# Block-causal attention and a gated MLP on one core: query block 8 ahead of its period, MLP groups listed by period, a sixth x buffer

## The chip, the cores and the metric

The kernel runs on one NeuronCore of a Trainium2 chip. A core has five engines that run side by side, each through its own queue in order: TensorE (PE, matrix products, its weight loads are shown as PEld), VectorE (DVE), ScalarE (ACT), GpSimd (POOL) and SyncE (SP, which issues all DMAs here). They meet at semaphores. The metric is the time of one execution on the device in microseconds; less is better.

## The reference

Eight batches of eight heads with 576 tokens and head dimension 64. Attention with a block-causal mask (blocks of 64 tokens) gives x, and a gated MLP with a spatial product follows:

```python
scores = np.where(block_i >= block_j, scale * q @ k.T, -1e9)
attn = exp(scores - max) / (sum + 1e-9)
x = attn @ v                                   # 576 x 512 per batch
h = np.maximum(x @ w_in, 0.0)                  # 512 -> 1024
u, v = h[..., :512], h[..., 512:]
v_n = (v - mean(v)) / sqrt(var(v) + 1e-6)
v_s = w_spatial @ v_n + b_spatial              # over the tokens, 576 x 576
out = (u * v_s) @ w_out
```

## The kernel before

The MLP's products are made in three passes: each float32 operand is split into a rounded part and a remainder (`hi` and `lo`, `gh` and `gl`, `vh` and `vl`), and hi x hi, hi x lo and lo x hi are added up in PSUM.

Two heads make a pair, four pairs a batch: 32 pairs. The four pairs of batch 0 run first in an older form (lines 819 to 843, "boot"), while the weights are loaded and split in the background. From pair 4 on one pass of the loop at line 874 is a period: the attention of pair g, the values product of pair g-1, and a share of the MLP of an earlier batch. Four periods make a batch.

Parts of a period:

- `scores_8` (L509): query block 8, the last 64 tokens of both heads. Two products (L515) into two PSUM banks, then `top` (the scaled minimum with mask on DVE, L484; the exponential on ACT, L491), `norm` (sums on DVE, L499 and L502; scaling on POOL, L505) and `turn_blocks(…, 8, 0)`: three transposes on DVE (L574 to L576) from the buffer `p8` into `pb`.
- `scores_run` (L521): the other query blocks 3, 2, 1, 0 of both heads: eight products (L536), eight `top`, the `norm`s, and the first turn. "Block 3" below is the first read of a score bank by DVE in it (L484 with 128x512).
- `av_pair` (L596) of the pair before: two banks of products of the turned probabilities `ptt` with `v` (L606), each copied out as `hi` by ACT (L403) and `lo` by DVE (L404).
- `turn_blocks` (L561): 32 x 32 transposes on DVE (L581, L583) from the p buffers into `pb`; `regroup` (L585): four DMAs for each head that bring `pb` into `ptt` (L592). There is one `pb` and one `ptt`.
- MLP groups, each an accumulation on PE in one of two PSUM banks: `v_group` (five a batch: four of 128 tokens, L639, and the tail, L650; with a statistics chain on DVE and ACT in later steps, L661 to L700), `u_group` (eight, L710), `sp_group` (the spatial product and the gating, eight, L734 to L747; L741 is the product with u), `out_group` (eight, L760; a copy on ACT, L766, and an output DMA, L767).

Six PSUM banks go round (`bank`, L466): 2 for block 8, 6 for the scores, 2 for `av` in each period. So the first `av` bank is that of block 3, and `av` may start once DVE has read it.

The order is written out by hand: `in_order` (L235) ties every new instruction to the one before it on its engine, so each engine, SP too, runs in the order of the program. `issue` (L851) makes a group's first step (its products and first evacuation) and then one further step of each earlier group that has steps left. Which groups run in a period is a matter of credit: each period adds `G_PAIR` (13.3), each group takes its cost, and `group` (L861) issues while credit is left. The order of the groups of a batch is that of `order` at L773, with the first half's gating behind the u groups, one u group, its output groups, then the second half. In a period block 8 comes first, then one group, then `scores_run`, `av_pair`, one group, the other turns with both regroups, and the other groups.

The x of a pair lies in one of five buffers (`xt_p`, L83), from its `av` until the last u group of its batch. The p buffers are six of 576 columns (L81), the output tiles four (L86).

Of the kernel before, what the change touches and what calls it, by code (L numbers as in the profile page):

```python
# [10 lines left out]
F32 = mybir.dt.float32  # L11
# [6 lines left out]
P = 128  # L18
# [22 lines left out]

G_V, G_VT, G_U, G_SP, G_OUT = 2.75, 1.83, 1.60, 1.86, 1.60
G_PAIR = (4 * G_V + G_VT + 8 * (G_U + G_SP + G_OUT)) / 4

TILES = [(2, 4), (0, 0), (0, 1), (1, 0), (1, 1), (0, 2), (0, 3), (1, 2), (1, 3)]
NT = len(TILES)  # L50
# [5 lines left out]
def kernel(  # L56
# [21 lines left out]
    const = ctx.enter_context(tc.tile_pool(name="const", bufs=1))  # L78
    raw_p = ctx.enter_context(tc.tile_pool(name="raw_p", bufs=2))
    v_p = ctx.enter_context(tc.tile_pool(name="v_p", bufs=2))  # L80
    p_p = ctx.enter_context(tc.tile_pool(name="p_p", bufs=6))  # L81
    pt_p = ctx.enter_context(tc.tile_pool(name="pt_p", bufs=1))
    xt_p = ctx.enter_context(tc.tile_pool(name="xt_p", bufs=5))  # L83
    st_p = ctx.enter_context(tc.tile_pool(name="st_p", bufs=6))
    ff_p = ctx.enter_context(tc.tile_pool(name="ff_p", bufs=1))
    o_p = ctx.enter_context(tc.tile_pool(name="o_p", bufs=4))  # L86
    ps_s = ctx.enter_context(tc.tile_pool(name="ps_s", bufs=3, space=PSUM))
    ps_t = ctx.enter_context(tc.tile_pool(name="ps_t", bufs=2, space=PSUM))
    ps_av = ctx.enter_context(tc.tile_pool(name="ps_av", bufs=1, space=PSUM))
# [142 lines left out]
    def pass_over():  # L232
        seen[0] = len(traced.instructions)
# [27 lines left out]
    boot = []  # L261
    BOOT_TAGS = [f"v{x}{c}" for x in "hl" for c in range(FULL)]

    def p_tile(b, nm, n):

        if b == 0 and n <= DH:
            boot.append(nm)
            k = (len(boot) - 1) % (len(BOOT_TAGS) + 2)
            if k < len(BOOT_TAGS):
                t = ff_p.tile([P, DH], F32R, tag=BOOT_TAGS[k], name=f"p_{nm}")  # L270
                return t.bitcast(F32)
        return p_p.tile([P, S], F32, tag="p", name=f"p_{nm}")

    banks = []

# [7 lines left out]
    def scores(b, pr, i):  # L283
        hd, t = TILES[i]
        nm = f"{b}_{pr}_{i}"
        nmax = st_p.tile([P, 2], F32, tag="nmax", name=f"nmax_{nm}")
        if t != 1:
            sums[0] = st_p.tile([P, 4], F32, tag="ssum", name=f"ssum_{nm}")
        ssum = sums[0]
        sc = 1 if t == 1 else 0  # L290
        pt = p_tile(b, nm, P * (t + 1))
        if hd < 2:
            n = P * (t + 1)
            js = slice(64 * hd, 64 * hd + 64)
            qs = slice(S + t * P, S + (t + 1) * P)
            ps = s_bank(nm)
            raw = raws[(b, pr)]
            mm(ps[:, :n], raw[js, qs], raw[js, :n], start=True, stop=True)
            nc.vector.tensor_tensor_reduce(
                out=pt[:, :n], in0=ps[:, :n], in1=mask[:, 512 - n:], scale=-0.125, scalar=BIG,  # L300
                op0=ALU.add, op1=ALU.min, accum_out=nmax[:, 0:1],
            )
            mx = nmax[:, 0:1]
        else:
            n = S
            for z in range(2):
                zs = slice(z * HT, (z + 1) * HT)
                ps = s_bank(f"{nm}_{z}")
                raw = raws[(b, pr)]
                mm(ps[:, :HT], raw[:, Q8:], raw[:, zs], start=True, stop=True)  # L310
                nc.vector.tensor_tensor_reduce(
                    out=pt[:, zs], in0=ps[:, :HT], in1=mask[:, :HT], scale=-0.125,
                    scalar=BIG if z == 0 else nmax[:, 0:1],
                    op0=ALU.add, op1=ALU.min, accum_out=nmax[:, z:z + 1],
                )
            mx = nmax[:, 1:2]
        nc.scalar.activation(
            pt[:, :n], pt[:, :n], AF.Exp, bias=mx, scale=-1.0, accum_out=ssum[:, sc:sc + 1]
        )
        ptiles[(b, pr, i)] = pt  # L320
        if t == 0:
            return
        nc.vector.tensor_scalar(
            out=ssum[:, 0:sc + 1], in0=ssum[:, 0:sc + 1], scalar1=EPS_SM, scalar2=None, op0=ALU.add
        )
        nc.vector.reciprocal(ssum[:, 2:3 + sc], ssum[:, 0:sc + 1])
        for k in range(sc, -1, -1):
            pk = ptiles[(b, pr, i - k)]
            nk = n if k == 0 else n - P
            nc.gpsimd.tensor_scalar(  # L330
                out=pk[:, :nk], in0=pk[:, :nk], scalar1=ssum[:, 2 + sc - k:3 + sc - k],
                scalar2=1.0, op0=ALU.mult, op1=ALU.mult,
            )
# [175 lines left out]
    def scores_8(b, pr):  # L509
        raw = raws[(b, pr)]  # L510
        st = stats[(b, pr)] = st_p.tile([P, 32], F32, tag="sst", name=f"sst_{b}_{pr}", bufs=3)
        parts = []
        for z in range(2):
            ps = bank(f"s8_{b}_{pr}_{z}")
            mm(ps[:, :HT], raw[:, Q8:], raw[:, z * HT:(z + 1) * HT], start=True, stop=True)  # L515
            parts.append(ps[:, :HT])
        top(st, 8, 0, p8[:, :S], parts)
        norm(st, [(8, 0, p8[:, :S])])
        turn_blocks(b, pr, 8, 0)

    def scores_run(b, pr):  # L521


        raw = raws.pop((b, pr))
        st = stats.pop((b, pr))
        ps = {}
        for t in (3, 2, 1, 0):
            for hd in range(2):
                js = slice(64 * hd, 64 * hd + 64)
                n = P * (t + 1)  # L530
                if t:
                    bk = bank(f"s{t}_{b}_{pr}_{hd}")
                    ps[(t, hd)] = bk[:, :n]
                    if t == 1:
                        ps[(0, hd)] = bk[:, n:n + P]
                mm(  # L536
                    ps[(t, hd)], raw[js, S + t * P:S + (t + 1) * P], raw[js, :n],
                    start=True, stop=True,
                )
        due = None  # L540
        for ts in ((3,), (2,), (1, 0)):
            tiles = []
            for hd in range(2):
                p = p_p.tile([P, S], F32, tag="p", name=f"p{ts[0]}_{b}_{pr}_{hd}")
                at = 0
                for t in ts:
                    n = P * (t + 1)
                    p_of[(b, pr, t, hd)] = p[:, at:at + n]
                    top(st, t, hd, p[:, at:at + n], [ps[(t, hd)]])
                    tiles.append((t, hd, p[:, at:at + n]))  # L550
                    at += n
            if due:
                norm(st, due)
            due = tiles
        turn_blocks(b, pr, 3, 0)
        norm(st, due)
# [60 lines left out]
    def moe(b):  # L617
# [149 lines left out]
            nc.sync.dma_start(outT[b, es, z * HT:(z + 1) * HT], o)  # L767
            yield

        vs = [(G_V if c < FULL else G_VT, lambda c=c: v_group(c)) for c in (0, 1, FULL, 2, 3)]  # L770
        us = [(G_U, lambda z=z, d=d: u_group(z, d)) for z in range(2) for d in range(ND)]

        order = "vuvuvuvuvuuuu" if b else "vvvuvuvuuuuuu"  # L773
        groups = [(vs if w == "v" else us).pop(0) for w in order]

        groups = groups[:-1] + [(G_SP, lambda d=d: sp_group(0, d)) for d in range(ND)] + groups[-1:]
        groups += [(G_OUT, lambda e=e: out_group(0, e)) for e in range(NO)]
        groups += [(G_SP, lambda d=d: sp_group(1, d)) for d in range(ND)]
        groups += [(G_OUT, lambda e=e: out_group(1, e)) for e in range(NO)]
        return groups  # L780


    pairs = [(b, pr) for b in range(B) for pr in range(NPAIR)]
# [2 lines left out]
    def run(gen):  # L786
        for _ in gen:
            pass
# [55 lines left out]

    queue = moe(0)
    credit = 0.0
    behind = []

    def issue(f):  # L851

        gen = f()
        next(gen)
        for e in list(behind):
            if next(e, e) is e:
                behind.remove(e)
        behind.append(gen)
        in_order()

    def group():  # L861
        nonlocal credit, n
        if queue and credit > 0.0:
            t, f = queue.pop(0)
            credit -= t
            issue(f)
            step_background(n)
            pass_over()
            n += 1
            return True  # L870
        return False

    pass_over()
    for g in range(NPAIR, len(pairs)):
        b, pr = pairs[g]
        n = max(n, g * NT)
        credit += G_PAIR
        scores_8(b, pr)
        in_order()
        group()  # L880
        scores_run(b, pr)
        av = av_pair(*pairs[g - 1]) if g > NPAIR else iter([])
        next(av, None)
# [2 lines left out]
        next(av, None)  # L886
        turn_blocks(b, pr, 2, 0)
        in_order()
        if g > NPAIR and pr == 0:
            queue += moe(b - 1)  # L890
        group()
        turn_blocks(b, pr, 1, 0)
        turn_blocks(b, pr, 0, 0)
        regroup(b, pr, 0)
        turn_blocks(b, pr, 2, 1)
        turn_blocks(b, pr, 1, 1)
        turn_blocks(b, pr, 0, 1)
        regroup(b, pr, 1)
        in_order()
        while group():  # L900
            pass
        if g + 1 < len(pairs):
            load_v(*pairs[g + 1])
        if g + 2 < len(pairs):
            load_pair(*pairs[g + 2])
        in_order()
    while queue:
        issue(queue.pop(0)[1])
    run(av_pair(*pairs[-1]))
    for _, f in moe(B - 1):  # L910
        issue(f)
    for e in behind:
        run(e)
# [64 lines left out]
```

## Time and profile before

| | us |
|---|---|
| median of 3 runs | 846.97 |
| lowest, highest | 844.66, 847.73 |
| profiled execution | 844.37 |
| its span, first to last instruction | 842.5 |
| PE busy in the span | 724.4 |
| granted clock of PE, mean | 0.947 |

The span is what the profile shows; 1.9 us of the profiled execution lie outside it. Times in views are counted from the start of the span. A view of waits gives, for each instruction group, how long its engine stood idle before it and what ended that, by semaphore events; a wait for several is put down to the last. A row of a timeline has the start, the length, engine, line, operation, tiles written and read, shapes and, in brackets, the idle time before it with what ended it. Matmuls overlap in the pipeline, so their lengths are longer than the distance of their starts. SP's rows show the issue of a DMA, not its transfer.

### The profile page before, as it was taken

The numbers are of one execution on the slowest core, as the hardware profiler recorded it, in microseconds if no ns is written. First come the engines' busy times: TensorE is split into PE (matmuls) and PEld (weight loads), VectorE is DVE, ScalarE is ACT, GpSimd is POOL, SyncE is SP. The second block draws the span as 40 slices with busy tenths as digits, with TensorE's granted clock in tenths as the row PEclk, the third lists the DMA queues.
The fourth block names the chain that finished last, engine by engine and source line by source line (L and its number), as shares of the span: only waits on it lengthen the run. The fifth ranks groups of instructions, "written<-read, shape, count | busy, mean of one in ns | idle before, by whom it ended". The sixth has DMA issues, their size and how long they took to land. (4 is left out here: it accounts for less than half of the span.)

```text
span 842.5 us, 14409 instructions
## 1 busy us (share of the span) xinstructions
PE 724.4 (86%) x4864; PEld 616.2 (73%) x4864; DVE 483.8 (57%) x1755; ACT 386.2 (46%) x1088; POOL 277.7 (33%) x428
## 2 busy tenths in 40 slices
PE   9998788888887987979789888888898888888997
PEld 5555577777776866868678767777677776787887
DVE  6967864566545665455665555565545657445331
ACT  6776633355433554335533345334543346334441
POOL 5775343233413333222333213332132322323121
PEclk9999799999999989999899998999999998999999
DMA  5544444541455404554225543245443453443001
GB/s 195 165 140 125 128 124 118 137 130 45 124 152 151 125 15 110 152 153 124 52 81 145 153 123 82 78 129 150 114 123 72 129 142 87 124 106 93 32 8 49
DMA packets 53660, 94.42 MB, mean 112 GB/s; under 512 B 5970, under 2 KB 43346, under 8 KB 53588
## 3 DMA queue, kind: packets, MB, share of 16 engines
q1 hardware_dynamic: 53588, 93.52, 40.8%
q8 instruction: 38, 0.62, 0.3%
q14 instruction: 34, 0.28, 0.1%
HBM read 38.18 MB, written 9.44 MB: 57 GB/s over the span
## 5 line engine op out<-in xcount | busy, mean ns | idle before, releaser
L505 POOL TENSOR_SCALAR p<-p,sst 128x384 f32<-128x384 f32 (+4 forms) x252 | 137.5, 560 | 312.4 <-DVE sst L502 272.9
L491 ACT ACTIVATE p<-p,sst 128x384 f32<-128x384 f32 (+4 forms) x252 | 144.4, 575 | 145.6 <-DVE sst L484 145.6
L606 PE MATMUL av<-ptt,v 128*64 128x32 f32 (+4 forms) x1120 | 113.1, 366 | 53.9 <-DVE sst L484 45.7
L606 PEld LDWEIGHTS av<-ptt,v 128*64 128x64 f32 x1120 | 100.1, 168 | 69.0 <-DVE sst L484 59.1
L484 DVE CUSTOM_DVE_ANT_0 p<-s,mask 128x384 f32<-128x384 f32 (+4 forms) x252 | 108.1, 478 | 44.8 <-PE s L515 42.7
L710 PE MATMUL mu<-x,wi_hi 128*128 128x288 f32 x512 | 111.1, 298 | 1.4 <-ACT vr L644 1.4
L760 PE MATMUL mo<-gh,wo_hi 128*128 128x288 f32 x256 | 63.9, 323 | 38.6 <-DVE u L741 21.6
L741 DVE TENSOR_TENSOR u<-ms,u 128x288 f32<-128x288 f32 x64 | 27.9, 436 | 111.0 <-PE ms L739 111.0
L639 PE MATMUL mv<-wi_hi,x 128*128 128x512 f32 x256 | 89.1, 409 | 2.9 <-ACT vr L644 2.2
L581 DVE STREAM_TRANSPOSE pb<-p 128x384 f32<-128x384 f32 (+1 forms) x224 | 91.4, 448 | 0.0
L734 PE MATMUL ms<-ws_hi,vh 128*128 128x288 f32 x256 | 80.7, 315 | 9.0 <-ACT vh L689 7.7
L710 PEld LDWEIGHTS mu<-x,wi_hi 128*128 128x128 f32 x512 | 84.6, 188 | 3.5 <-ACT vr L644 1.9
L690 POOL TENSOR_TENSOR vl<-vr,vh 128x512 fp32r<-128x512 f32 x32 | 41.0, 1280 | 138.5 <-ACT vh L689 81.0
L734 PE MATMUL ms<-ws_hi,vl 128*128 128x288 f32 x256 | 76.2, 298 | 5.7 <-POOL vl L690 5.7
L760 PEld LDWEIGHTS mo<-gh,wo_hi 128*128 128x128 f32 x256 | 46.1, 208 | 45.0 <-issue 24.5
L734 PE MATMUL ms<-ws_lo,vh 128*128 128x288 f32 x256 | 75.3, 294 | 0.0
L710 PE MATMUL mu<-x,wi_lo 128*128 128x288 f32 x256 | 69.8, 295 | 0.0
L536 PE MATMUL s<-raw 64*128 64x512 f32 (+1 forms) x448 | 68.6, 443 | 0.0
L766 ACT COPY o<-mo 128x288 f32<-128x288 f32 x64 | 25.6, 400 | 93.7 <-PE mo L760 69.4
L536 PEld LDWEIGHTS s<-raw 64*128 64x128 f32 x448 | 41.2, 186 | 28.3 <-issue 19.3
L760 PE MATMUL mo<-gl,wo_hi 128*128 128x288 f32 x256 | 61.0, 322 | 0.0
L639 PEld LDWEIGHTS mv<-wi_hi,x 128*128 128x128 f32 x256 | 49.3, 193 | 14.9 <-ACT vr L644 2.4
(127 smaller groups left out, 1379.4 us busy)
## 6 DMA issues: line engine op xcount, KB each, us to landing
ptt<-pb SPq DMA_DIRECT2D x224, 200.0 KB, 4.1
raw<-qk SPq DMA_DIRECT2D x31, 608.0 KB, 5.2
v<-v SPq DMA_DIRECT2D x32, 320.0 KB, 4.0
outT<-o SPq DMA_DIRECT2D x64, 144.0 KB, 2.9
rwi<-w_in SPq DMA_DIRECT2D x8, 512.0 KB, 3.9
rwo<-w_out SPq DMA_DIRECT2D x4, 512.0 KB, 3.6
rws<-w_spT SPq DMA_DIRECT2D x4, 288.0 KB, 2.8
rwt<-w_spT SPq DMA_DIRECT2D x2, 144.0 KB, 2.8
```

Of the source, the lines that this page charges most:

```text
L484: nc.vector.tensor_tensor_reduce(out=p[:, at:at + n], in0=ps, in1=mk, scale=-0.125, scalar=BIG if m == 0 else st[:, k:k + 1], op0=ALU.add, ...
L491: nc.scalar.activation(p, p, AF.Exp, bias=mx, scale=-1.0, accum_out=st[:, 10 + k:11 + k])
L505: nc.gpsimd.tensor_scalar(out=p, in0=p, scalar1=st[:, k:k + 1], scalar2=1.0, op0=ALU.mult, op1=ALU.mult)
L536: mm(ps[(t, hd)], raw[js, S + t * P:S + (t + 1) * P], raw[js, :n], start=True, stop=True,)
L581: nc.vector.transpose(to(hd * XH + 32 * t, [[P, m], *dims] if m > 1 else dims), p[:, :m * P])
L606: mm(to[js, :, PA - C_N[c]:], vt[:, c, js], ptt[:, 2 * z:2 * z + 2, at:at + C_N[c]], start=(c == 0), stop=(c == 4),)
L639: mm(ps, xs[k][:, j, cs], w[:, k, DH:], start=(n == 0), stop=(n == 3 * NC - 1),)
L690: nc.gpsimd.tensor_tensor(out=vl, in0=vr, in1=vh.bitcast(F32), op=ALU.subtract)
L710: mm(ps[:, :HT], w[:, k, ds], xs[k][:, j, zs], start=(n == 0), stop=(n == 3 * NC - 1),)
L734: mm(ps[:, :HT], a[:, ds], w[:, k, zs], start=(n == 0), stop=False)
L741: nc.vector.tensor_tensor(out=uz, in0=ps[:, :HT], in1=uz, op=ALU.mult)
L760: mm(ps[:, :HT], w[:, k, es], a[:, k, :], start=(n == 0), stop=(n == 3 * ND - 1),)
```

## The change

Four things are changed.

1. `scores_8` becomes a generator of three steps: products and `top`; `norm`; the turn into `pb`. The next pair's block 8 takes one step behind each of the last four groups of a period (the fourth only ends the generator). The first pair's block 8 runs ahead of the loop.
2. `moe` returns five lists instead of one queue with costs. A period takes one of them; the first period of a batch takes the last list of the batch before it and the first of its own. The gating groups of a half end a period, and the output groups that use them begin the next. The other turns stand behind the first group, the two regroups behind the second and the third.
3. Six x buffers for five.
4. To make room: p buffers by size (two of 512, four of 384 columns), boot's block 8 in `p8`, boot's p tiles in a round of eleven for ten, three output tiles for four.

```diff
-    p_p = ctx.enter_context(tc.tile_pool(name="p_p", bufs=6))
+    p_p = ctx.enter_context(tc.tile_pool(name="p_p", bufs=1))
-    xt_p = ctx.enter_context(tc.tile_pool(name="xt_p", bufs=5))
+    xt_p = ctx.enter_context(tc.tile_pool(name="xt_p", bufs=6))
-    o_p = ctx.enter_context(tc.tile_pool(name="o_p", bufs=4))
+    o_p = ctx.enter_context(tc.tile_pool(name="o_p", bufs=3))
...
+    def p_big(nm):
+        return p_p.tile([P, 512], F32, tag="p3", name=nm, bufs=2)
+
+    def p_small(nm):
+        return p_p.tile([P, 384], F32, tag="p21", name=nm, bufs=4)
...
         top(st, 8, 0, p8[:, :S], parts)
+        yield
         norm(st, [(8, 0, p8[:, :S])])
+        yield
         turn_blocks(b, pr, 8, 0)
+        yield
...
-        order = "vuvuvuvuvuuuu" if b else "vvvuvuvuuuuuu"
-        groups = [(vs if w == "v" else us).pop(0) for w in order]
-
-        groups = groups[:-1] + [(G_SP, lambda d=d: sp_group(0, d)) for d in range(ND)] + groups[-1:]
...
+        if b == 0:
+            first = [[*vs[0:3], us[0], vs[4]], [vs[3], *us[1:6]], us[6:] + sp[0]]
+        else:
+            first = [
+                [vs[0], vs[4], us[0]], [vs[1], us[1], vs[2], us[2], vs[3], us[3]], us[4:] + sp[0]
+            ]
+        return [*first, out[0] + sp[1], out[1]]
...
     pass_over()
+    ahead = scores_8(*pairs[NPAIR])
+    run(ahead)
+    mlp = moe(0)
+    rest = []
     for g in range(NPAIR, len(pairs)):
         b, pr = pairs[g]
         n = max(n, g * NT)
-        credit += G_PAIR
-        scores_8(b, pr)
-        in_order()
-        group()
         scores_run(b, pr)
         av = av_pair(*pairs[g - 1]) if g > NPAIR else iter([])
...
         turn_blocks(b, pr, 2, 0)
         in_order()
-        if g > NPAIR and pr == 0:
-            queue += moe(b - 1)
-        group()
-        turn_blocks(b, pr, 1, 0)
-        turn_blocks(b, pr, 0, 0)
-        regroup(b, pr, 0)
-        turn_blocks(b, pr, 2, 1)
-        turn_blocks(b, pr, 1, 1)
-        turn_blocks(b, pr, 0, 1)
-        regroup(b, pr, 1)
+        if pr == 0:
+            if g > NPAIR:
+                mlp = moe(b - 1)
+            groups, rest = rest + mlp[0], mlp[-1]
+        else:
+            groups = mlp[pr]
+        ahead = scores_8(*pairs[g + 1]) if g + 1 < len(pairs) else iter([])
+        for i, f in enumerate(groups):
+            issue(f)
+            if i == 0:
+                turn_blocks(b, pr, 1, 0)
+                turn_blocks(b, pr, 0, 0)
+                turn_blocks(b, pr, 2, 1)
+                turn_blocks(b, pr, 1, 1)
+                turn_blocks(b, pr, 0, 1)
+            if i in (1, 2):
+                regroup(b, pr, i - 1)
+            if i >= len(groups) - 4:
+                next(ahead, None)
         in_order()
-        while group():
-            pass
...
-    while queue:
-        issue(queue.pop(0)[1])
+    for f in rest[:2]:
+        issue(f)
     run(av_pair(*pairs[-1]))
-    for _, f in moe(B - 1):
+    for f in rest[2:] + sum(moe(B - 1), []):
         issue(f)
```

More of the change, by code (lines that the diff above doesn't have):

```diff
@@ L40, in x_at @@
     return 32 * t + (P * c if c < 3 else 176)
-G_V, G_VT, G_U, G_SP, G_OUT = 2.75, 1.83, 1.60, 1.86, 1.60
-G_PAIR = (4 * G_V + G_VT + 8 * (G_U + G_SP + G_OUT)) / 4
 TILES = [(2, 4), (0, 0), (0, 1), (1, 0), (1, 1), (0, 2), (0, 3), (1, 2), (1, 3)]
@@ L262, with p_tile @@
     BOOT_TAGS = [f"v{x}{c}" for x in "hl" for c in range(FULL)]
[L264 to L272, printed above, removed]
+    def p_big(nm):
+        return p_p.tile([P, 512], F32, tag="p3", name=nm, bufs=2)
+    def p_small(nm):
+        return p_p.tile([P, 384], F32, tag="p21", name=nm, bufs=4)
+    def p_tile(nm, n):
+        if n == S:
+            return p8
+        boot.append(nm)
+        k = (len(boot) - 1) % (len(BOOT_TAGS) + 3)
+        if k < len(BOOT_TAGS):
+            t = ff_p.tile([P, DH], F32R, tag=BOOT_TAGS[k], name=f"p_{nm}")
+            return t.bitcast(F32)
+        return (p_small if n <= 384 else p_big)(f"p_{nm}")
     banks = []
@@ L290, in scores @@
         sc = 1 if t == 1 else 0
-        pt = p_tile(b, nm, P * (t + 1))
+        pt = p_tile(nm, P * (t + 1) if hd < 2 else S)
         if hd < 2:
@@ L543, in scores_run @@
             for hd in range(2):
-                p = p_p.tile([P, S], F32, tag="p", name=f"p{ts[0]}_{b}_{pr}_{hd}")
+                p = (p_big if ts[0] == 3 else p_small)(f"p{ts[0]}_{b}_{pr}_{hd}")
                 at = 0
@@ L768, in out_group @@
             yield
-        vs = [(G_V if c < FULL else G_VT, lambda c=c: v_group(c)) for c in (0, 1, FULL, 2, 3)]
-        us = [(G_U, lambda z=z, d=d: u_group(z, d)) for z in range(2) for d in range(ND)]
-        order = "vuvuvuvuvuuuu" if b else "vvvuvuvuuuuuu"
-        groups = [(vs if w == "v" else us).pop(0) for w in order]
-        groups = groups[:-1] + [(G_SP, lambda d=d: sp_group(0, d)) for d in range(ND)] + groups[-1:]
[L777 to L780, printed above, removed]
+        vs = [lambda c=c: v_group(c) for c in range(FULL + 1)]
+        us = [lambda z=z, d=d: u_group(z, d) for z in range(2) for d in range(ND)]
+        sp = [[lambda z=z, d=d: sp_group(z, d) for d in range(ND)] for z in range(2)]
+        out = [[lambda z=z, e=e: out_group(z, e) for e in range(NO)] for z in range(2)]
+        if b == 0:
[5 more added lines that the diff above has]
+        return [*first, out[0] + sp[1], out[1]]
     pairs = [(b, pr) for b in range(B) for pr in range(NPAIR)]
@@ L843 @@
         n += 1
-    queue = moe(0)
-    credit = 0.0
     behind = []
     def issue(f):
+        nonlocal n
         gen = f()
@@ L859, in issue @@
         in_order()
[L861 to L871, printed above, removed]
+        step_background(n)
+        pass_over()
+        n += 1
     pass_over()
+    ahead = scores_8(*pairs[NPAIR])
+    run(ahead)
+    mlp = moe(0)
+    rest = []
     for g in range(NPAIR, len(pairs)):
```

## The prediction

> **What bounds the kernel now.** I read the page first, then the waits of TensorE (PE), then the engines in chosen windows, then the timelines of one batch. The page says that PE is the busiest engine by far, and that all other engines have room:
>
> ```profile
> span 842.5 us, 14409 instructions
> PE 724.4 (86%) x4864; PEld 616.2 (73%) x4864; DVE 483.8 (57%) x1755; ACT 386.2 (46%) x1088; POOL 277.7 (33%) x428
> ```
>
> PE is idle for 842.5 - 724.4 = 118 us. The view of who waited for whom, on PE alone, says where:
>
> ```profile
> PE av L606 <- DVE sst L484: 45.7, 22, 5.7
> PE mo L760 <- DVE u L741: 21.6, 14, 2.5
> PE mo L760 <- ACT gh L744: 17.0, 15, 2.1
> PE ms L734 <- ACT vh L689: 7.7, 7, 1.2
> PE ms L734 <- POOL vl L690: 5.7, 7, 0.8
> ```
>
> The columns are total, times and longest. The first row is the product of probabilities and values (`av`, L606): its PSUM bank comes free when VectorE (DVE) has read the score block 3 from it (L484). The next two are the output group, which waits for the gate halves. The last two are a gating product that comes too soon after its normalised operand. Together they make 97.7 us.
>
> Idle time costs twice. The windows (length, busy time of PE, PEld, DVE, ACT, POOL, then the granted clock) show it:
>
> ```profile
> 370.10:472.50 102.40, 87.53 (x601) 76.44 (x600) 58.80 (x217) 45.01 (x129) 30.59 (x50) 0.93 0.43 115
> 397.20:403.40 6.20, 2.41 (x17) 1.44 (x16) 4.20 (x14) 2.49 (x6) 0.75 (x1) 0.94 0.00 0
> 403.40:409.20 5.80, 5.79 (x41) 4.74 (x41) 5.54 (x25) 4.75 (x17) 3.27 (x6) 0.50 0.00 0
> 455.00:458.10 3.10, 3.06 (x41) 2.90 (x41) 3.04 (x17) 3.08 (x10) 0.98 (x2) 1.00 0.04 13
> 477.20:481.90 4.70, 4.70 (x41) 4.40 (x41) 4.39 (x21) 4.68 (x17) 2.21 (x4) 0.64 0.04 12
> ```
>
> The first row is one batch of four periods, 102.4 us. The same 40 `av` matmuls take 3.1 us at clock 1.00, 5.8 at 0.50 behind a long idle stretch, and 4.7 at 0.64. A batch at 0.93 loses about 102.4 x 0.07 = 7 us to the clock.
>
> How much PE needs without waits comes from its timeline. The groups of the last batch run nearly alone:
>
> ```profile
> 782.30 0.50 PE L639 MATMUL mv<-wi_hi,x 128*128 128x512 f32 x1
> ...
> 839.02 0.29 PE L760 MATMUL mo<-gl,wo_hi 128*128 128x288 f32 x1
> ...
> PE mo L760 <- ACT gh L744: 1.1, 1, 1.1
> PE ms L734 <- POOL vl L690: 0.8, 1, 0.8
> PE ms L734 <- ACT vh L689: 0.7, 1, 0.7
> ```
>
> That is 57.0 us. The last three rows are the waits of PE in the same stretch, 2.6 us, of which the pipeline hides some more: about 54 for the 37 groups of a batch. A pair's attention on PE:
>
> ```profile
> 448.94 1.13 PE L515 MATMUL s<-raw 128*128 128x288 f32 x4
> 449.70 0.51 PE L734 MATMUL ms<-ws_hi,vh 128*128 128x288 f32 x1
> ...
> 451.85 2.43 PE L536 MATMUL s<-raw 64*128 64x512 f32 x16
> 455.04 3.09 PE L606 MATMUL av<-ptt,v 128*64 128x288 f32 x40 [0.77 <-DMA raw<-qk]
> ```
>
> Block 8 keeps PE for 0.76 us (448.94 to 449.70), the matmul behind it starts some 0.3 slower, scores take 2.43 and `av` 3.1: 6.6 a pair, 26.4 a batch. PE's own need is 54 + 26.4 = 80.4 us a batch, against 102.4. The most that any order can win is 22 us a batch.
>
> **The change, part by part.**
>
> *Block 8 ahead.* Why `av` waits is seen on DVE in the worst period:
>
> ```profile
> 399.87 0.58 DVE L574 STREAM_TRANSPOSE pb<-p 128x384 f32<-128x384 f32 x1 [0.95 <-POOL p L505]
> ...
> 402.69 0.66 DVE L484 CUSTOM_DVE_ANT_0 p<-s,mask 128x512 f32<-128x512 f32 x1
> ...
> 403.41 0.74 PE L606 MATMUL av<-ptt,v 128*64 128x288 f32 x1 [3.81 <-DVE sst L484]
> ```
>
> DVE works in order. Before it may read block 3 (402.69) it must turn block 8 (399.87), for which it waits through ACT's exponential and POOL's scaling. `av` starts 0.7 after that read. After the change block 8 is scored, scaled and turned among the last four groups of the period before, so that chain lies beside MLP matmuls. The instructions are the same, none is added; 45.7 us of waits lose their reason.
>
> What is late next is the turn itself. It writes the single buffer `pb`, which the eight regroup DMAs (L592) of the previous pair must have read. They now stand behind groups 1 and 2 on SP's queue, and the turn is placed two groups earlier. So a loop is closed: read of block 3, turns, eight DMAs, their landing, turn of block 8, what stands behind it on DVE, next read of block 3. Its terms:
>
> ```profile
> 454.30 0.67 DVE L484 CUSTOM_DVE_ANT_0 p<-s,mask 128x512 f32<-128x512 f32 x1
> ...
> 462.37 1.59 DVE L581 STREAM_TRANSPOSE pb<-p 128x256 f32<-128x256 f32 x5
> 463.89 0.41 DVE L741 TENSOR_TENSOR u<-ms,u 128x288 f32<-128x288 f32 x1
> 464.80 0.46 DVE L745 TENSOR_TENSOR gl<-u,gh 128x288 fp32r<-128x288 f32 x1 [0.50 <-ACT gh L744]
> ```
> ```profile
> 463.05 6.56 SPq L592 DMA_DIRECT2D ptt<-pb  x8
> 469.71 2.99 SPq L767 DMA_DIRECT2D outT<-o  x4
> ...
> DMA to landing us min/median/max: 3.1/4.1/5.9
> ```
> ```profile
> 392.01 0.14 DVE L666 TENSOR_SCALAR st<-st 128x1 f32<-128x1 f32 x1
> ...
> 392.95 0.68 DVE L661 BATCH_NORM_STATS2 st<-vr 64x6 f32<-64x512 f32 x1
> 393.66 0.17 DVE L662 BATCH_NORM_AGGREGATE st<-st 64x2 f32<-64x6 f32 x1
> ```
>
> Read of block 3 to first regroup DMA: 463.05 - 454.30 = 8.75, with one L741 (0.41) in it that the new order has not there: 8.4. First to last DMA issue: 7/8 of 6.56, 5.7. Landing: the median is 4.1 and the longest 5.9; the last of eight queues behind the others, I take 4.4. Turn of block 8: three transposes, 0.9. Hops between engines: 1 us a batch. Then what differs by period, by the new lists:
> - Period 0 (out x4, v, v tail, u): one output DMA stands between the two regroups (2.99/4 = 0.75). Behind the turn on DVE come the first v group's statistics chain (392.01 to 392.95: 0.9) and the tail's statistics (0.85). 8.4 + 5.7 + 0.75 + 4.4 + 0.9 + 1.75 = 21.9.
> - Period 1 (v, u three times): the tail's chain (0.9) ahead of the turns, one statistics pair (0.85) behind: 21.2.
> - Period 2 (u x4, gating x4): a chain (0.9) ahead; behind the turn the last product and its halves, 463.89 to 465.26, 1.4: 21.7.
> - Period 3 (out x4, gating x4): 0.75 and 1.4: 21.6.
>
> The sum is 86.4, plus 1 for hops. PE needs 80.4 / 4 = 20.1 in the mean, so the loop and not PE sets the period, and PE still idles some 1.5 us ahead of an `av`. Period 0 has the longest loop and no gating group, so the longest idle time, I take it to be over 2 us; and in before a gap of 2.24 ended in the 4.70 window at clock 0.64 above:
>
> ```profile
> 477.18 1.28 PE L606 MATMUL av<-ptt,v 128*64 128x288 f32 x6 [2.24 <-DMA raw<-qk]
> ```
>
> So I add one such loss a batch, 4.7 - 3.1 = 1.6, which reaches the loop through the v group whose statistics chain stands ahead of the turns. 86.4 + 1 + 1.6 = 89 us a batch. Bounds: 80.4 + 2 if the loop does not bind; up to 104 if the DMAs start as late as in the worst period, below.
>
> The Trainium skill (TensorE: Matmul & The Clock Gate, section "HAM oscillation — how this bites in real kernels") asks only that PE idle no longer than about 3.4 us at a stretch; the row of 2.24 speaks against that here. By the rule the 1.6 would go.
>
> *Groups by period.* The gating products of a half now end a period, and the output groups that use them start after the next scores and `av` (5.5 us of PE). L741, gh and gl need 1.4 to 2 us, so the 38.6 us of waits at L760 go within the periods; if that cover went, they would be back. The last v group gets a whole period and four u groups before its use: 13.4 us of waits at L734 go. All this makes PE shorter, which the loop above already allows for; it is worth nothing beyond it. In the last batch, which has no periods, output follows gating directly in both halves: one wait of about 1.5 more.
>
> *Six x buffers, smaller p buffers, three o buffers.* The sixth x buffer lets the second pair's x be written while the u groups still read the last batch; with five, `av` would wait for groups queued behind it on the same engine. p buffers have as many tiles as a pair uses. The fourth output copy of a run now needs the landing of the first:
>
> ```profile
> outT<-o SPq DMA_DIRECT2D x64, 144.0 KB, 2.9
> ```
>
> It lands 2.9 us after its issue, and three output groups lie between, so nothing is lost on PE; if the issue were held behind a regroup, one landing a run would show. Bounds 0 to 2.9 us a run, I take 0.
>
> *Sum.* Starts of scores (first of a batch, first of the last one, last period):
>
> ```profile
> 167.78 0.70 PE L536 MATMUL s<-raw 64*128 64x512 f32 x2
> ...
> 677.31 0.70 PE L536 MATMUL s<-raw 64*128 64x512 f32 x2
> ...
> 759.03 0.70 PE L536 MATMUL s<-raw 64*128 64x512 f32 x2
> ```
>
> Five batches, 509.5, become 5 x 89 = 445: -64.5. Three periods, 81.7, become 21.9 + 21.2 + 21.7 + 1.6 + 0.7 = 67.1: -14.6. The first batch also splits weights; I take -8, of 0 to -13. Behind 759.03 stand two gating and four output groups more than before (10 us), with some 4 us less of waits: +6. Together -81: 844.4 (profiled execution, span 842.5) becomes 763.5. The median of the runs shown, 847.0, lies 0.3% above that execution; I forecast 765.
>
> **The rivals.**
> 1. *The loop, without the cold window*: 1.6 less in some six batches, 755. This is what the skill's rule gives. For it: the residual idle is under 3 us. Against it: the row of 2.24.
> 2. *PE is the bound.* The regroup loop turns out shorter, because landing or issue overlaps more than I allow. 82.4 a batch: 5 x 19.5 + 20 + 11 - 6 = 122 less, 722 to 725. Against it: the DMA terms are measured, and the single `pb` stays.
> 3. *The regroup starts late.* In the worst period it did:
>
> ```profile
> 414.86 6.57 SPq L592 DMA_DIRECT2D ptt<-pb  x8
> ```
>
> That is 12.2 after the read of block 3 at 402.69, not 8.4, since statistics chains held DVE. Two such periods a batch: 89 + 7.6 = 96.6, about 810.
> 4. *Slower than before.* The same in all four periods, since DVE, stuck at the turn, carries L741 and the statistics late into the next period: 89 + 15.2 = 104.2 a batch and a cold window of 1.6 in three more: some 109, so 5 x 7 + 0 + 6 more, about 880. It decides from a first regroup DMA later than 12.3 after the read of block 3.
> 5. *The change only moves the wait*: DVE stands at the turn as long as PE stood at `av`, 845.
>
> **How the numbers follow.** Forecast 0.47; rival 1 0.16; rival 2 0.14; rival 3 0.15; rival 4 0.04; rival 5 0.04. The range reaches from rival 2 to rival 3, 715 to 812; the forecast's own is 750 to 785. A measurement tells 0.5% from no change. Faster: the forecast and rivals 1 to 3, 0.92; same: rival 5, 0.04; slower: rival 4, 0.04.
>
> **What would show it.** Right: the waits of L606 for L484 fall to some 1 to 2 us a period but not to nothing; the waits of DVE's L574 are ended by the regroup DMAs and grow; the waits of L760 and L734 go except in the last batch; periods lie at 21 to 24 us with clock above 0.97. Rival 2: L574 waits for POOL as now, and periods come down to 20. Rivals 3 and 4: the first L592 of a period comes over 12 us after the read of block 3. The forecast is wrong if the turn does not wait for the landing, or if DVE has work ahead of block 3 that I did not list.

## The result, and the profile after

| | before | after |
|---|---|---|
| median, us | 845.8 (844.3 to 847.7, 4 runs) | 781.0 (776.4 to 782.0, 4 runs) |
| ratio | | 0.922 (0.918 to 0.926) |
| profiled execution, us | 844.4 | 780.7 |
| its span, us | 842.5 | 778.9 |
| clock of PE, mean | 0.947 | 0.965 |

The change saves 65 us where 81 were forecast. Below, the four periods of a batch are called the first to the fourth; the prediction counts them from 0. In the changed kernel the read of block 3 is L487 (L484 before), `av` L612 (L606), the output group L766 (L760), the gating L747, L750 and L751 (L741, L744 and L745); in the experiments the numbers differ by a few. The page of the changed kernel (span; then busy time, share and instructions of each engine):

```profile
span 778.9 us, 14424 instructions
PE 695.1 (89%) x4864; PEld 598.6 (77%) x4864; DVE 480.6 (62%) x1755; ACT 382.4 (49%) x1088; POOL 276.5 (36%) x428
```

Each engine runs as many instructions as before; DVE's busy time hardly moves (483.8 to 480.6). PE is idle for 83.8 us instead of 118, and busy for 29 us less; as an estimate, the clock accounts for 17 of these 29 (0.053 of 842.5 us against 0.035 of 778.9). The view of waits on PE alone, in the changed kernel (total, times, longest):

```profile
PE av L612 <- DVE sst L487: 63.9, 25, 9.5
PE mu L716 <- ACT u L721: 10.0, 7, 5.9
PE mo L766 <- ACT gh L750: 3.2, 3, 1.1
```

The waits of the output groups for the gate halves fell from 38.6 to 3.2 us, those of the gating product (13.4) are gone; new is a wait of the u groups, 10.0 us, 5.9 of it once. But `av` waits longer than before, 63.9 us against 45.7 (and 8.3 that the view put down to a DMA). In the five batches in the middle it idles 2.1 us a period in the mean, where it was 1.9 before. Why is seen in the waits of DVE:

```profile
DVE pb L580 <- DMA v<-v: 37.6, 21, 4.4
...
DVE pb L580 <- DMA outT<-o: 6.4, 3, 2.6
...
DVE pb L580 <- DMA ptt<-pb: 3.4, 2, 1.8
```

L580 is the turn of block 8 (L574 before). Before, most of its waits were for POOL, some 0.95 us each; now 26 of 28 turns end a wait for DMAs, 47 us together. By the trace these DMAs take turns on the same semaphores as the regroup's, so the name behind the arrow changes. The turn for the first period of one batch began at 346.28; the timeline of DVE in the changed kernel shows what follows it:

```profile
346.28 0.58 DVE L580 STREAM_TRANSPOSE pb<-p 128x384 f32<-128x384 f32 x1 [2.60 <-DMA v<-v]
346.78 0.27 DVE L581 STREAM_TRANSPOSE pb<-p 128x128 f32<-128x128 f32 x1
346.97 0.27 DVE L582 STREAM_TRANSPOSE pb<-p 128x128 f32<-128x128 f32 x1
347.17 0.42 DVE L747 TENSOR_TENSOR u<-ms,u 128x288 f32<-128x288 f32 x1
348.08 0.46 DVE L751 TENSOR_TENSOR gl<-u,gh 128x288 fp32r<-128x288 f32 x1 [0.50 <-ACT gh L750]
348.46 0.68 DVE L487 CUSTOM_DVE_ANT_0 p<-s,mask 128x512 f32<-128x512 f32 x1
```

From the turn to the read of block 3 go 2.2 us, and PE, whose scores began at 344.96, gets its bank only at 349.2. The previous read of block 3 was at 326.25, so this period of the loop took 348.46 - 326.25 = 22.2 us.

SP's timeline for the same period, with the four DMAs of each head and the output DMAs between them:

```profile
332.41 1.85 SPq L773 DMA_DIRECT2D outT<-o  x2
334.69 3.14 SPq L598 DMA_DIRECT2D ptt<-pb  x4
337.93 0.55 SPq L773 DMA_DIRECT2D outT<-o  x1
338.58 3.71 SPq L598 DMA_DIRECT2D ptt<-pb  x4
```

First regroup DMA 8.4 us behind the read (334.69 - 326.25), as forecast. By the trace's record of landings the last of them landed at 346.0, 0.27 us ahead of the turn. One batch, from the windows (length, busy time of PE, PEld, DVE, ACT, POOL, granted clock, DMA share and GB/s):

```profile
344.96:436.56 91.60, 83.24 (x602) 73.89 (x601) 58.41 (x216) 44.52 (x129) 30.36 (x50) 0.96 0.49 128
```

91.6 us, where the kernel before took 102.4 and 89 were forecast.

### The profile page after: what moved, and what is told of

It is laid out like the page before. It is cut to its first block, busy times and chain, and to the rows that moved or that the text cites. A ratio compares the mean times of both kernels' runs of the same rounds, so it can differ in the third digit from the quotient of the medians.

```text
span 778.9 us, 14424 instructions
## 1 busy us (share of the span) xinstructions
PE 695.1 (89%) x4864; PEld 598.6 (77%) x4864; DVE 480.6 (62%) x1755; ACT 382.4 (49%) x1088; POOL 276.5 (36%) x428
## 5 line engine op out<-in xcount | busy, mean ns | idle before, releaser
L612 PE MATMUL av<-ptt,v 128*64 128x32 f32 (+4 forms) x1120 | 106.1, 350 | 64.2 <-DVE sst L487 63.9
L612 PEld LDWEIGHTS av<-ptt,v 128*64 128x64 f32 x1120 | 94.8, 160 | 77.7 <-DVE sst L487 69.3
L487 DVE CUSTOM_DVE_ANT_0 p<-s,mask 128x384 f32<-128x384 f32 (+4 forms) x252 | 108.1, 478 | 9.7 <-PE s L518 9.3
L751 POOL TENSOR_TENSOR gl<-u,gh 128x288 fp32r<-128x288 f32 x48 | 38.6, 803 | 162.1 <-ACT gh L750 162.1
L747 DVE TENSOR_TENSOR u<-ms,u 128x288 f32<-128x288 f32 x64 | 28.7, 449 | 98.1 <-PE ms L745 98.1
L645 PE MATMUL mv<-wi_hi,x 128*128 128x512 f32 x256 | 87.0, 401 | 0.0
L740 PE MATMUL ms<-ws_hi,vh 128*128 128x288 f32 x256 | 78.5, 306 | 0.0
L542 PE MATMUL s<-raw 64*128 64x512 f32 (+1 forms) x448 | 71.6, 450 | 0.9 <-DVE x L407 0.9
L750 ACT CAST gh<-u 128x288 fp32r<-128x288 f32 x64 | 25.9, 428 | 89.2 <-DVE u L747 89.2
L766 PE MATMUL mo<-gh,wo_hi 128*128 128x288 f32 x256 | 57.1, 302 | 3.2 <-ACT gh L750 3.2
L772 ACT COPY o<-mo 128x288 f32<-128x288 f32 x64 | 25.5, 398 | 63.9 <-PE mo L766 55.6
```

The costliest lines, as they stand in the source:

```text
L487: nc.vector.tensor_tensor_reduce(out=p[:, at:at + n], in0=ps, in1=mk, scale=-0.125, scalar=BIG if m == 0 else st[:, k:k + 1], op0=ALU.add, ...
L542: mm(ps[(t, hd)], raw[js, S + t * P:S + (t + 1) * P], raw[js, :n], start=True, stop=True,)
L612: mm(to[js, :, PA - C_N[c]:], vt[:, c, js], ptt[:, 2 * z:2 * z + 2, at:at + C_N[c]], start=(c == 0), stop=(c == 4),)
L645: mm(ps, xs[k][:, j, cs], w[:, k, DH:], start=(n == 0), stop=(n == 3 * NC - 1),)
L740: mm(ps[:, :HT], a[:, ds], w[:, k, zs], start=(n == 0), stop=False)
L751: (nc.vector if dc == ND - 1 else nc.gpsimd).tensor_tensor(out=gl[:, dc, :], in0=uz, in1=gh[:, dc, :].bitcast(F32), op=ALU.subtract)
```

## The experiments

Each was timed on one chip beside the kernel before; ratios are to that, with their 95% intervals. The theory: the period is a loop from the read of block 3 through turns, regroup, landing and turn of block 8 back to the read.

**The turn of block 8 behind the reads.** In the changed kernel its step is moved into `scores_run`, with nothing else:

```diff
         norm(st, [(8, 0, p8[:, :S])])
         yield
-        turn_blocks(b, pr, 8, 0)
-        yield
...
             due = tiles
+        turn_blocks(b, pr, 8, 0)
         turn_blocks(b, pr, 3, 0)
```

> The changed kernel with one step moved: the turn of block 8 (three transposes into pb) stands behind the reads of all score banks of its own period, no longer ahead of the last group of the period before. Loop theory (the read of block 3 waits, through the turn, for the landing of the eight regroup DMAs): the wait no longer stands ahead of the reads, so the idle time ahead of av falls from about 2 us a period to under 0.5 except behind the tail group, periods come down to what PE needs, 20 to 21 us, and the whole to 715 to 735 us. Rival (what holds the reads is the other work of VectorE, statistics chains and gating products): the idle time stays at 1 to 2 us a period and the time at 765 or more.

Measured: 720.8 us, 0.850 (0.849 to 0.852), as the loop theory has it. The waits of PE in that run, and one batch of its windows:

```profile
PE av L611 <- DVE sst L487: 16.6, 14, 4.6
PE mu L715 <- ACT u L720: 10.0, 7, 5.9
PE ms L739 <- ACT u L720: 5.1, 6, 1.1
```
```profile
398.51:481.94 83.43, 79.92 (x602) 70.16 (x601) 57.24 (x216) 44.26 (x129) 30.50 (x50) 1.00 0.53 140
```

`av` waits 16.6 us for 63.9, the clock in that batch is 1.00, and the batch takes 83.4 us. Three transposes, moved behind the reads on one queue, are worth 60 us. The move takes their work (0.9 us a period) off the path along with the wait, so the 60 us are not the wait for the landing alone.

**Block 8 back in its own period**, the lists and buffers kept:

```diff
-    ahead = scores_8(*pairs[NPAIR])
-    run(ahead)
...
+        run(scores_8(b, pr))
         scores_run(b, pr)
...
-            if i >= len(groups) - 4:
-                next(ahead, None)
```

> The changed kernel with block 8 put back to the start of its own period, all three steps ahead of the other scores; the lists of groups by period, the six x buffers and the place of the regroups stay. Theory that block 8 ahead is what won the time: av waits again for block 8's chain, 3 to 5 us a period with half clock behind it, periods of 24 to 26 us, 810 to 840 us in all. Rival (the new lists won it): within 10 us of the changed kernel, 781.

Measured: 834.7 us, 0.985 (0.982 to 0.988). Its waits of PE:

```profile
PE av L612 <- DVE sst L487: 84.4, 27, 6.5
PE s L542 <- DVE sst L487: 8.4, 8, 2.5
PE mo L766 <- ACT gh L750: 3.2, 3, 1.1
```

The lists alone do take away the waits of L766 (3.2), but the wait of `av` grows to 84.4: with no MLP group between block 8 and the scores, the chain lies bare. So the 13 us are what is left of the 38.6 + 13.4 us of waits that the lists remove, once the bare chain is paid for. The lists with a group left between block 8 and the scores were not tried.

**Block 8 ahead alone**, in the kernel before with its queue, one group still ahead of the scores. Not shown are the `yield`s of `scores_8` and `groups_left`, which counts the groups that the credit still allows:

```diff
+    run(scores_8(*pairs[NPAIR]))
...
-        scores_8(b, pr)
-        in_order()
         group()
         scores_run(b, pr)
...
         while group():
-            pass
+            if groups_left() < 4:
+                next(ahead, None)
+        run(ahead)
```

> The kernel before with block 8 alone ahead: its three steps stand behind the last four groups of the period before; the queue with credit, five x buffers and the turns and regroups where they were. Theory that block 8 ahead won most: the waits of av fall to 1 to 2 us a period, the waits of the output groups for the gate halves (some 38 us in all) stay, 785 to 810 us. Rival (the lists won it): 835 to 847 us.

Measured: 800.9 us (790.5 to 802.8), 0.946 (0.944 to 0.948): most of the gain, with the waits of the output groups nearly as they were (19.9 and 16.6 us in its profile, of an execution of 790.5 us). By these two runs the parts win 13 and 47 us, together 65. In that profile `av` waits only 14.6 us for block 3, though the turn of block 8 stands for DMAs there too, 53.9 us in 13 waits. There one MLP group lies between the turn and the scores. Whether that alone would hide the turn's wait in the changed kernel was not tried.

**The turns ahead of the first group.** The second period of a batch took 23 to 26 us, the first regroup DMA coming 12.2 us behind the read in four of six. DVE's timeline of the changed kernel shows what stood before the turns:

```profile
371.25 0.65 DVE L487 CUSTOM_DVE_ANT_0 p<-s,mask 128x512 f32<-128x512 f32 x1
...
378.50 0.56 DVE L587 STREAM_TRANSPOSE pb<-p 128x384 f32<-128x384 f32 x1
378.99 0.10 DVE L672 TENSOR_SCALAR st<-st 64x1 f32<-64x1 f32 x1
382.13 0.26 DVE L676 TENSOR_SCALAR st<-st 64x1 f32<-64x1 f32 x1 [3.04 <-ACT st L671]
...
382.80 1.60 DVE L587 STREAM_TRANSPOSE pb<-p 128x256 f32<-128x256 f32 x5
```

From 378.99 to 382.80 are 3.8 us. The chain's work is under 1 us, but DVE stands 3.04 us in it for ACT, which stands behind the first group's matmuls, and these behind an `av` at half clock (rows on the clock below). The edit:

```diff
         for i, f in enumerate(groups):
-            issue(f)
             if i == 0:
                 turn_blocks(b, pr, 1, 0)
...
+            issue(f)
```

> The changed kernel with the five turns of blocks 2, 1 and 0 ahead of the first group of a period instead of behind it. Theory on the long second period (25 us, first regroup DMA 12.2 us behind the read of block 3): a statistics chain of that first group's step holds VectorE ahead of the turns. Then the first regroup DMA comes 8.4 us behind the read in every period, the second period falls from 25 to some 21.5 us, the third by 1, and the whole by 25 to 30 us to 750 to 757. Rival (the second period is long because PE is at half clock there): first regroup DMA still at 11 us or more, time within 8 us of 781.

Measured: 771.1 us, 0.911 (0.908 to 0.914). The first regroup DMA now came 8.4 us behind the read in the second period (455.43 to 463.84 in the batch below), so the cause of the late start is shown; but the gain is 10 us, not 25 to 30. DVE's timeline of this run at the end of such a period:

```profile
473.41 0.13 DVE L672 TENSOR_SCALAR st<-st 128x1 f32<-128x1 f32 x1
475.71 0.27 DVE L676 TENSOR_SCALAR st<-st 128x1 f32<-128x1 f32 x1 [2.16 <-ACT st L671]
...
476.87 0.58 DVE L580 STREAM_TRANSPOSE pb<-p 128x384 f32<-128x384 f32 x1 [0.39 <-DMA raw<-qk]
```

The turn hardly waits there any more (0.39). Ahead of it DVE stands for another statistics chain, that of a v group near the period's end. The period came down only to 23.4 us in the mean, and what still lengthens it goes with the clock. In one of six batches the `av` of that period ran at full clock, and the period took 22.0 us, near the 21.5 expected. In the others that `av` took 4.6 to 5.8 us for 3.1, and the period 23.1 to 24.4. The `av` of the first two of these batches, from the windows of that run:

```profile
184.40:187.50 3.10, 3.10 (x41) 2.94 (x41) 2.98 (x17) 3.06 (x10) 0.97 (x2) 1.00 0.00 0
272.75:278.54 5.79, 5.79 (x41) 4.76 (x41) 5.44 (x24) 4.76 (x17) 2.87 (x5) 0.52 0.02 3
```

So the rival, half clock, seems to have its share in the length of the period, though the late start of the regroup is gone in all six. This is a comparison of batches within one run; no run took the clock's share away by itself.

**Both moves**, this one and the turn of block 8 behind the reads.

> Both moves at once: the turn of block 8 behind the score reads, and the five other turns ahead of the period's first group. If the loop over the landing is gone already with the first move, the second has nothing left to win: 717 to 724 us, like the first alone (720.8). If the regroup's start still matters: 705 to 715.

Measured: 732.9 us, 0.867 (0.866 to 0.869): 12 us worse than the first alone. The third period of a batch grew (23.2 to 24.9 us from scores to scores, for 21.7 to 22.1), and in its waits of PE the gating products now wait:

```profile
PE av L611 <- DVE sst L487: 17.4, 14, 4.8
PE ms L739 <- ACT u L720: 13.7, 6, 2.6
```

13.7 us for 5.1. With the landing no longer in the loop, turns that come earlier win nothing. By the order on DVE they push back the last v group's statistics, which the gating needs; that this is the whole cause was not tried. Neither of the two outcomes that were expected came.

**The second head's regroup in smaller pieces**, on the changed kernel and on the one with the late turn:

```diff
+        cut = (0, XH // 2, XH) if hd else (0, XH)
         for a in range(4):
-            nc.sync.dma_start(ptts[(b, pr)][:, a, xs], pb[32 * a:32 * a + 32, :, xs])
+            for lo, up in zip(cut, cut[1:]):
+                xs = slice(hd * XH + lo, hd * XH + up)
+                nc.sync.dma_start(ptts[(b, pr)][:, a, xs], pb[32 * a:32 * a + 32, :, xs])
```

> The changed kernel with each of the four regroup DMAs of the second head cut in two of half the width: the same bytes, four DMAs more to issue, about 0.6 to 0.8 us each. Loop theory (regroup issue and landing set the period): every period of the 27 grows by 2 to 3.3 us, with more half clock, 835 to 875 us. Rival (the DMAs are hidden; the changed kernel's periods are set by VectorE or PE): within 8 us of 781.

> The same cut of the second head's regroup DMAs, on the kernel whose turn of block 8 stands behind the score reads. There the landing has some 4 us to spare before the turn asks for it, so by the loop theory the four DMAs more cost nothing: 719 to 728 us. Rival (smaller pieces load the DMA engines or SP so that everything slows): as many us more as in the changed kernel, 770 or more.

Measured: 793.1 us, 0.939 (0.935 to 0.942), on the changed kernel, which has 0.922; 721.5 us, 0.854 (0.852 to 0.856), on the one with the late turn, which has 0.850. The sign is that of the loop theory, 12 us against 1, but 12 us is far from the 54 to 94 that were expected, and outside the rival's 8. SP's timeline of the first:

```profile
339.15 3.19 SPq L600 DMA_DIRECT2D ptt<-pb  x4
342.44 0.55 SPq L775 DMA_DIRECT2D outT<-o  x1
343.09 5.53 SPq L600 DMA_DIRECT2D ptt<-pb  x8
```

Eight pieces take 5.53 us to issue where four took 3.71. Yet the last landing, counted from the read of block 3, moved only from 20.1 to 20.7 us in the fourth period and from 22.1 to 22.4 in the second (means over seven batches of each profile, where the landing is recorded): the smaller last piece lands sooner after its issue. That fits a landing set by the data moved more than by the number of issues, but whether the transfers or SP's pace set it was not separated.

**Regroups one group later**, on the changed kernel:

```diff
-            if i in (1, 2):
-                regroup(b, pr, i - 1)
+            if i in (2, 3):
+                regroup(b, pr, i - 2)
```

> The changed kernel with the regroups behind the third and fourth group of a period, not the second and third. In the two periods of a batch that begin with output groups SP then has the third output DMA ahead of the first regroup, so that the first regroup DMA comes about 1.5 us later (9.9 us behind the read of block 3 for 8.45); in the other two SP has nothing else to do and nothing moves. Loop theory: those two periods grow by about 1.5 us each, 13 of them, 796 to 808 us in all. Rival (the landing does not bind): 776 to 786.

Measured: 799.2 us (790.5 to 805.9), 0.947 (0.942 to 0.952). In its profile, of an execution of 790.5 us, the first regroup DMA of the fourth period came 9.8 us behind the read for 8.4, and that period took 23.0 to 23.5 us from read to read for 22.2. In the first period it came as late, and that period took 23.0 to 23.7 us, once 26.8, for 22.4 to 23.0. So a delay of the regroup by 1.4 us lengthens these periods by 0.6 to 1 us, less than the 1.5 expected: the landing binds, in the changed kernel, as the theory has it.

**What is left with the late turn.** There `av` still idled 1.48 us in the second period of each batch, behind statistics, the tail's last. Two orders of the first period were tried, out, out, v, tail, out, out, u and then the tail ahead of the v group:

```diff
-            groups, rest = rest + mlp[0], mlp[-1]
+            groups, rest = rest[:2] + mlp[0][:2] + rest[2:] + mlp[0][2:], mlp[-1]
...
-                [vs[0], vs[4], us[0]], [vs[1], us[1], vs[2], us[2], vs[3], us[3]], us[4:] + sp[0]
+                [vs[4], vs[0], us[0]], [vs[1], us[1], vs[2], us[2], vs[3], us[3]], us[4:] + sp[0]
```

The first run has only the upper of the two edits.

> The kernel with the turn of block 8 behind the score reads, and the first period of a batch in the order out, out, v, v tail, out, out, u instead of four out first, so that both statistics chains are over before the next scores. What is left there is an idle time of 1.48 us ahead of av in the second period of each batch, behind those chains; it should fall to under 0.3, six times 1.2 to 1.5 us: 711 to 714 us. Rival (that idle time is of the ScalarE exponentials or of the banks): 719 to 723.

Measured: 734.2 us, 0.869 (0.867 to 0.871), worse by 13 us. DVE's timeline of that run, ahead of the scores of a second period:

```profile
429.13 0.20 DVE L683 TENSOR_SCALAR st<-st 64x1 f32<-64x1 f32 x1
430.22 0.42 DVE L700 CAST vs_b<-vr 64x512 fp32r<-64x512 f32 x1 [0.88 <-ACT vr L688]
430.67 0.69 DVE L702 TENSOR_TENSOR vs_a<-vr,vs_b 64x512 fp32r<-64x512 f32 x1
431.39 0.69 DVE L487 CUSTOM_DVE_ANT_0 p<-s,mask 128x512 f32<-128x512 f32 x1
```

The tail's last step had come to stand right ahead of the read, and it waits for ACT. `av` idled 2.49 us there, and its matmuls then took 4.7 to 4.8 us for 3.1, at half clock in part. The steps of a group fall due one per later group, so an order of groups is also an order of their late steps.

> As the run with the tail group early, but the tail ahead of the first v group: out, out, v tail, v, out, out, u. In that run the tail's last step (two casts on VectorE that wait for ScalarE behind the last u group's evacuation) came to stand right ahead of the score reads. Here that step falls on the last output group, and the step beside the last u group is the v group's, which has no VectorE work. Theory that VectorE's statistics steps at the period's end are what is left: the idle time ahead of av in the second period of a batch falls to under 0.3, no cold window there, and the whole to 708 to 714 us. Rival: 720 or more.

Measured: 706.7 us, 0.835 (0.833 to 0.837), the best of the kernels here, a little under the range that was expected. `av` idles 0.52 us in that period, not under 0.3, and no half clock follows; one batch of its windows:

```profile
392.22:473.19 80.97, 79.71 (x602) 69.59 (x601) 57.69 (x216) 44.28 (x129) 30.56 (x50) 1.00 0.55 144
```

81.0 us a batch, against the 80.4 that the prediction gave as PE's own need.

## Why the prediction came out as it did

- **Block 8's chain held `av`, and the move lifts that.** Right: put back, 834.7 us; alone, 800.9. But `av` idles as long as before in the changed kernel, 2.1 us a period where some 1.5 were forecast, as the landing now holds it.
- **The landing closes a loop that sets the period.** Right, and shown from three sides: the turn's waits are ended by DMAs, a regroup 1.4 us later lengthens two of the four periods by 0.6 to 1, and with the turn behind the reads the wait is gone and the batch comes down to 83.4 us. Of the first side, the view itself names the regroup in only two of the 26 waits. Rival 2, PE as the bound, is what the kernel becomes with the late turn, not what the change made of it.
- **Sizes of the loop.** The first period was put at 21.9 us, without hops and clock, and took 22.4 to 23.0; the third 21.7 and took 21.7 to 22.7; the fourth 21.6 and took 22.1 to 22.3. The second was put at 21.2, or 22.8 with the 1.6 for the clock, and took 23.1 to 25.8, 24.7 in the mean. This is the mis-sized step: the chain ahead of the turns was priced at its work, 0.9 us, and cost 3.8, for it waits for ACT, which waits for the first group's matmuls. The first regroup DMA came 12.2 us behind the read for the 9.3 of the prediction's sum. Of these 2.9 us about 1.7 go with the half clock. In one of six batches the `av` of the second period ran at full clock (463.20 to 466.30 below); there DVE stood 1.36 us for ACT instead of 3.04, and the first DMA came 10.6 us behind the read:

```profile
471.72 0.27 DVE L676 TENSOR_SCALAR st<-st 64x1 f32<-64x1 f32 x1 [1.36 <-ACT st L671]
```

So the path by which the prediction let the clock reach the loop, through that v group's chain, is the one seen; what it left out of the chain's price is some 1.3 us of waiting at full clock. Rival 3 had the price of 12.2, but for two periods a batch; it came in one. Of the signs given, periods of 21 to 24 us held for all but the second.
- **The clock.** One loss of 1.6 us a batch was added. The window of the five middle batches of the changed kernel gives it:

```profile
159.02:617.12 458.10, 412.26 (x3001) 365.79 (x3000) 292.14 (x1080) 222.25 (x645) 151.85 (x250) 0.97 0.48 127
```

At 0.97 a loss of 458.1 x 0.03 = 14 us, 2.7 a batch where 1.6 were added. The row also has the batch, 458.1 / 5 = 91.6.
- **The sum.** From the profiles: five batches 458.1 us (445 forecast), the last three periods 71.9 (67.1), the first batch -8.8 (-8), and behind the last scores 89.9 (83.5 + 6). The 17 us that are missing lie in the steady periods alone.
- **The lists.** Their waits went as forecast (38.6 to 3.2, 13.4 to 0), and with block 8 in its old place they win 13 us, the bare chain paid for. In the prediction they were worth nothing beyond a shorter PE; in a kernel whose `av` waits anyway, that is nearly so.
- **Buffers.** That a sixth x buffer and a third o buffer cost or win nothing by themselves was not tried apart: by the order of the program the sixth x buffer is needed, for with five `av` would wait for groups behind it.

The clock deserves rows of its own. In the changed kernel, three stretches of idle time ahead of `av` and the `av` behind them, from its windows:

```profile
365.90:372.00 6.10, 2.52 (x18) 1.50 (x17) 4.25 (x15) 0.91 (x3) 0.00 (x0) 1.00 0.71 215
372.00:376.70 4.70, 4.70 (x41) 4.39 (x41) 4.38 (x21) 4.70 (x17) 2.22 (x4) 0.64 0.01 3
457.60:463.20 5.60, 2.40 (x17) 1.44 (x16) 4.11 (x15) 0.91 (x3) 0.00 (x0) 1.00 0.76 225
463.20:466.30 3.10, 3.07 (x41) 2.91 (x41) 2.98 (x17) 3.03 (x10) 0.94 (x2) 1.00 0.01 3
391.80:396.40 4.60, 2.45 (x18) 1.49 (x17) 3.10 (x11) 2.18 (x7) 2.85 (x3) 1.00 0.84 243
396.40:401.00 4.60, 4.60 (x40) 4.02 (x40) 4.38 (x21) 4.60 (x17) 2.12 (x4) 0.63 0.03 10
```

Idle for 3.58 us (6.10 less busy 2.52) PE fell to 0.64 in the next stretch, idle for 3.2 it did not, idle for 2.15 it did. So length alone does not decide. At 0.64 over 4.7 us, half clock held for 2 x 0.36 x 4.7 = 3.4 us.

What decides shows in the trace's clock records. In every run here, apart from what the two ends cut off, half clock comes in pieces of 3.41 us or twice that, and within a run all of them begin whole multiples of 3.41 us apart. Cut along these edges, the same three gaps read:

```profile
369.13:372.54 3.41, 0.57 (x5) 0.52 (x7) 3.20 (x14) 0.54 (x1) 0.00 (x0) 1.00 0.47 166
372.54:375.95 3.41, 3.41 (x26) 3.20 (x24) 3.26 (x17) 3.41 (x14) 1.47 (x3) 0.50 0.02 5
457.87:461.28 3.41, 2.13 (x16) 1.17 (x13) 2.03 (x7) 0.78 (x3) 0.00 (x0) 1.00 0.93 260
461.28:464.69 3.41, 1.46 (x21) 1.40 (x21) 3.31 (x13) 1.42 (x4) 0.00 (x0) 1.00 0.24 99
393.02:396.43 3.41, 1.26 (x13) 0.84 (x10) 2.45 (x9) 1.52 (x3) 1.63 (x2) 1.00 0.79 260
396.43:399.84 3.41, 3.41 (x24) 2.89 (x26) 3.35 (x17) 3.41 (x12) 1.36 (x2) 0.50 0.05 13
```

In the first pair PE idled 2.84 us within one window (3.41 less busy 0.57), in the third 2.15, and the next window ran at half clock. The gap of 3.2 us was split by an edge into 1.28 and 1.95, and `av` ran at full clock. Over the twelve traces, from 150 us on, a window at full clock with under 1.7 us of idle time was never followed by half clock, one with 2.0 or more always; between them both occur. In the kernel before, the gap of 2.24 us from which the prediction took its 1.6 comes in six batches. Behind five of them `av` ran at 0.58 or 0.59, behind one (172.45) at 1.00.

The Trainium skill (TensorE: Matmul & The Clock Gate, Part 1: The HAM clock gate) says that activity is judged in free-running windows of 3413 ns. The pieces of 3.41 us above agree. Its rule of thumb, no idle gaps over about 3.4 us (section "HAM oscillation — how this bites in real kernels"), is too lax here: 2.15 us in this kernel and 2.49 in the run with the tail early were followed by half clock.

## What to carry to other kernels

When a step is moved ahead to lift a wait, look for the buffer that it writes and for the last reader of that buffer: here three transposes, ready early, stood on an in-order queue waiting for DMAs, and held work behind them that needed nothing of the sort. A step that may wait belongs behind the work that something else waits for, even if its inputs are ready sooner; moving it was worth nearly as much again (60 us) as the whole change (65). And price a step in an in-order queue by what it waits for, not by its work: a statistics chain of 0.9 us cost 3.8, as the engine that it asked was itself behind matmuls, which ran in part at half clock.

## What the runs showed of the hardware that was not expected

- Half clock came in pieces of 3.41 us on a grid that is fixed within a run, and PE's idle time within one window of that grid decided: from 2.0 us on it always followed, under 1.7 never. So gaps of 2.15 and 2.49 us were followed by half clock, and a gap of 3.2 us that an edge split was not (rows above).
- Cutting four of eight DMAs in two added some 1.8 us of issue but moved the last landing by 0.3 to 0.7 us only.
